# The four sums of each pair of token rows on GpSimd instead of VectorE, in a kernel of three chained matrix products

## The chip, the core and the metric

The kernel runs on one core of a Trainium2 chip. Five engines work side by side, each through its own queue of instructions, in order: TensorE (PE; matmuls, 128 by 128), VectorE (DVE), ScalarE (ACT), GpSimd (POOL) and SyncE (SP, which here only issues DMAs). GpSimd issues DMAs too. The metric is the device time of one execution in microseconds (us).

## What is computed

x is 2048 tokens by 640 channels, fp32. The reference takes the layer norm of x, the real part of its two-dimensional Fourier transform by DFT matrices, and an MLP across the tokens with 1728 hidden units; the sum of x and both is the output:

```python
def _A_ref(x, dft_seq_re, dft_seq_im, dft_hid_re, dft_hid_im):
    a = jnp.einsum("bsd,ed->bse", x, dft_hid_re)
    b = jnp.einsum("bsd,ed->bse", x, dft_hid_im)
    return jnp.einsum("ts,bse->bte", dft_seq_re, a) - jnp.einsum("ts,bse->bte", dft_seq_im, b)

def _B_ref(x, w1, b1, w2, b2):
    h = _layernorm(x, axis=-1)
    u = _gelu(jnp.einsum("bsd,sf->bdf", h, w1) + b1)
    return (jnp.einsum("bdf,fs->bds", u, w2) + b2).transpose(0, 2, 1)

x = A_x
xn = _layernorm(x, axis=-1)
return x + _A_ref(xn, ...) + _B_ref(xn, B_w1, B_b1, B_w2, B_b2)
```

## The kernel before

**Products.** Every fp32 product is made of three matmuls (`three`, lines 158 to 164): each operand is cut into a rounded high part, which ScalarE writes (`high`, line 150), and the remainder, which VectorE subtracts (`low`, line 153); high by high, high by low and low by high are added in PSUM. Besides, blocks of two by two are multiplied with seven products in place of eight, so that sums and differences of blocks are operands as well.

**Stages.** `first_columns` and `columns` multiply the normalized rows of x by the DFT matrices along the tokens and store the result y to DRAM (`store_y`, lines 488 to 492, DMAs issued by GpSimd). `hidden` multiplies y by the DFT along the channels, `up` and `down` are the MLP. The stage of the change is the first, up to about 190 us.

**The fixed operand.** In the first stage the rows of x are the operand that stays in SBUF. There are two halves of eight blocks of 128 token rows. Block q and block q + 4 of a half are a pair, q from 0 to 3, and each pair gets a tile of operands with high and low parts (`fixed[h][q]`; in the lists below n_119 to n_122 for pairs 0 to 3 of the first half, n_1045, n_1266, n_1452 and n_1672 for the second). Of the 640 channels the first 512 go in two quarters of Q = 256 through the seven products, which need four sums of a pair, each of 128 by 256 (`sums_of_rows`, lines 329 to 367). With `row` for block q and `lower` for block q + 4, and 0 and 1 for the quarter, they are, all in place: lower1 = row1 + lower1 (job1, line 342), lower1 = lower1 - row0 (job2), lower0 = lower0 - lower1 (job3), row1 = row0 - row1 (job4); the last three go through the helper `sub` of line 156. After each sum ScalarE copies its high part (`hi`), and at the start of the next job VectorE takes the remainder (`lo`). The second sum overwrites what the first one's remainder reads, so it stands behind that remainder; the others wait for earlier sums alone.

**The order.** Every engine's instructions stand in the order in which the program writes them (`tc.manual_schedule`). The start is a list of words; from step 6 on `turn_of(i, ...)` writes one turn for each step i: loads, reads of PSUM banks, the ScalarE cut of the piece of step i + 2 (a piece is a 128 by 512 block of the DFT matrix, the operand that moves; three buffers), copies of PSUM banks to c tiles and their stores, `jobs` taken from a queue, the VectorE remainder of that piece, more jobs, and last the matmuls of step i. The sums of the first half stand in that queue from step 6 in the order (pair, job) 00 01 10 11 02 12 20 21 30 31 22 32 03 13 and so on, one or two a turn by a table of numbers (`JOBS_AT`). In what follows, a turn is named by its i: turn 11 has the third sum of pair 1, turn 12 the first two of pair 2, turn 14 the first two of pair 3, turn 20 the third sums of pairs 2 and 3. The piece that is cut at the head of turn i + 1, right behind such a turn's last job, belongs to step i + 3. Those of the second half follow from about 110 us on, three neighbouring turns with one sum each behind a first.

Of the kernel before, what the change touches and what calls it, by code (L numbers as in the profile page):

```python
# [77 lines left out]
def fnet_plus_mixer(  # L78
# [30 lines left out]
    nc = tc.nc  # L109
# [39 lines left out]
    def high(hi, src):  # L149
        nc.scalar.activation(hi, src, AF.Copy)  # L150

    def low(lo, src, hi):
        nc.vector.tensor_sub(lo, src, hi.bitcast(F32))  # L153

    def sub(to, a, b):
        nc.vector.tensor_sub(to, a, b)  # L156
# [163 lines left out]
    def part(a, which, i, n=1):  # L320
        return a[:, which, at_slot[i] : at_slot[i] + n * Q]
# [7 lines left out]
    def sums_of_rows(h, q, row, lower, apart=False):  # L329


        def a(of, i):
            return of()[:, i * Q : (i + 1) * Q]

        def hi(i, src):
            high(part(fixed[h][q], 0, i), src)

        def lo(i, src):
            low(part(fixed[h][q], 1, i), src, part(fixed[h][q], 0, i))

        def job1():
            nc.vector.tensor_add(a(lower, 1), a(row, 1), a(lower, 1))
            hi(3, a(lower, 1))

        def job2():
            lo(3, a(lower, 1))
            sub(a(lower, 1), a(lower, 1), a(row, 0))
            hi(4, a(lower, 1))

        def job3():  # L350
            lo(4, a(lower, 1))
            sub(a(lower, 0), a(lower, 0), a(lower, 1))
            hi(5, a(lower, 0))

        def job4():
            lo(5, a(lower, 0))
            sub(a(row, 1), a(row, 0), a(row, 1))
            if not apart:
                job5()

        def job5():
            hi(6, a(row, 1))

        def job6():
            lo(6, a(row, 1))

        return [job1, job2, job3, job4] + [job5] * apart + [job6]


# [934 lines left out]
```

## Time and profile before

| | |
|---|---|
| median of 3 runs | 866.72 us (866.56 to 866.78) |
| span of the profiled execution | 865.1 us, first to last instruction; 1.6 us less than the median |
| TensorE, weight loads | busy 860.7 us, 789.6 us |
| VectorE, ScalarE | busy 695.2 us, 523.0 us |
| GpSimd | busy 158.8 us, of it 195 DMAs issued |
| granted TensorE clock | 1.000 over the span |

The profile gives no time of the profiled execution other than its span. The page gives busy times by engine, the chain of work that ended last and the costliest groups of instructions by line. Besides it the trace answers by view: who waited for whom; a timeline of one engine in a stretch of time (start, duration, engine, line, operation, what is written and read, and in brackets the idle time before and what ended it; "x2" are two instructions in a row, with the time from the first's start to the last's end); busy times by windows. Instructions of ScalarE and VectorE that follow each other overlap by about a tenth of a microsecond in these rows.

### The profile page before, as it was taken

To read this page: it belongs to the slowest core of one execution; us is meant where nothing else is said; L and a number is where in the kernel's file an instruction comes from. 1 tells how busy PE (TensorE), PEld (TensorE's weight loads), DVE (VectorE), ACT (ScalarE), POOL (GpSimd) and SP (SyncE) were. 2 spreads that over 40 slices of the span, in tenths; PEclk is the share of its full clock that TensorE was granted. 3 is DMA by queue.
4 is the path that set the end of the run, shared out by engine and by line. 5 is a ranking of instruction groups with operands and counts; after the bars stand their busy time and mean duration, and the time that the engine had idled before them with its cause. 6 is when DMAs were issued, how large, how long until landed. Compare 5 with 4: busy or idle time off the path is not lost.

```text
span 865.1 us, 13904 instructions
## 1 busy us (share of the span) xinstructions
PE 860.7 (99%) x4899; PEld 789.6 (91%) x4899; DVE 695.2 (80%) x1177; ACT 523.0 (60%) x968; POOL 158.8 (18%) x215
## 2 busy tenths in 40 slices
PE   9999999999999999999999999999999999999998
PEld 6888888888888888889999999999999999999998
DVE  7898868758767888677877788888679978987887
ACT  5765576763555555547565556676667866555654
POOL 2222131210020211122110101111312221101211
PEclk9999999999999999999999999999999999999999
DMA  9949596695382746869576766665687689766776
GB/s 337 366 103 268 186 245 235 160 292 151 94 191 29 199 102 135 212 107 200 125 167 157 163 138 196 189 173 162 142 185 176 146 241 244 183 141 126 157 170 149
DMA packets 90293, 154.44 MB, mean 179 GB/s; under 512 B 9008, under 2 KB 37424, under 8 KB 89968
## 3 DMA queue, kind: packets, MB, share of 16 engines
q0 software_dynamic: 25008, 57.52, 36.1%
q1 hardware_dynamic: 64928, 95.80, 34.0%
q8 instruction: 38, 0.62, 0.3%
q10 hardware_dynamic: 288, 0.25, 0.1%
q14 instruction: 31, 0.25, 0.1%
HBM read 99.96 MB, written 58.82 MB: 184 GB/s over the span
## 4 chain that ended last, share of the span: by engine, by line
PE 99%; DMA 1%; SPq 0%; ACT 0%; DVE 0%; issue 0%; DVEq 0%
PE psum L161 32%; PE psum L162 32%; PE psum L164 31%; PE psum L515 3%; DMA pieces<-in_dft_seq 1%; ACT piece L150 0%; SPq L503 0%; SPq L539 0%; DVE pair L954 0%; DVEq L1300 0%
## 5 line engine op out<-in xcount | busy, mean ns | idle before, releaser
L153 DVE TENSOR_TENSOR piece<-pieces,piece 128x512 fp32r<-128x512 f32 (+4 forms) x496 | 327.2, 660 | 129.8 <-ACT piece L150 125.2
L150 ACT ACTIVATE piece<-pieces 128x512 fp32r<-128x512 f32 (+3 forms) x472 | 295.3, 626 | 224.6 <-PE psum L164 143.0
L161 PE MATMUL psum<-piece,n 128*128 128x512 f32 x540 | 210.3, 389 | 0.0
L164 PE MATMUL psum<-piece,n 128*128 128x512 f32 x540 | 210.3, 389 | 0.0
L162 PE MATMUL psum<-piece,n 128*128 128x512 f32 x540 | 210.3, 389 | 0.0
L162 PE MATMUL psum<-sup,piece 128*128 128x320 f32 x392 | 120.9, 309 | 0.0
L162 PE MATMUL psum<-sdown,piece 128*128 128x320 f32 x392 | 120.9, 309 | 0.0
L161 PE MATMUL psum<-sup,piece 128*128 128x320 f32 x392 | 120.9, 309 | 0.0
L161 PE MATMUL psum<-sdown,piece 128*128 128x320 f32 x392 | 120.9, 309 | 0.0
L162 PEld LDWEIGHTS psum<-piece,n 128*128 128x128 f32 x540 | 101.4, 188 | 21.1
L161 PEld LDWEIGHTS psum<-piece,n 128*128 128x128 f32 x540 | 101.4, 188 | 20.9
L164 PEld LDWEIGHTS psum<-piece,n 128*128 128x128 f32 x540 | 101.4, 188 | 20.9
L156 DVE TENSOR_TENSOR pieces<-pieces 128x512 f32<-128x512 f32 (+3 forms) x142 | 111.9, 793 | 3.0
L164 PE MATMUL psum<-sup,piece 128*128 128x320 f32 x368 | 113.9, 310 | 0.0
L164 PE MATMUL psum<-sdown,piece 128*128 128x320 f32 x368 | 113.9, 310 | 0.0
L492 POOL DMA_DIRECT2D y<-c x65 | 56.0, 898 | 255.2 <-DVE c L691 154.0
L164 PE MATMUL psum<-shid,piece 128*128 128x320 f32 x280 | 86.7, 310 | 0.0
L162 PE MATMUL psum<-shid,piece 128*128 128x320 f32 x280 | 86.7, 309 | 0.0
L161 PE MATMUL psum<-shid,piece 128*128 128x320 f32 x280 | 86.6, 309 | 0.0
L161 PEld LDWEIGHTS psum<-sdown,piece 128*128 128x128 f32 x392 | 73.6, 188 | 0.0
L161 PEld LDWEIGHTS psum<-sup,piece 128*128 128x128 f32 x392 | 73.6, 188 | 0.0
L162 PEld LDWEIGHTS psum<-sup,piece 128*128 128x128 f32 x392 | 73.6, 188 | 0.0
(135 smaller groups left out, 1107.2 us busy)
## 6 DMA issues: line engine op xcount, KB each, us to landing
pieces<-in_dft_seq SPq DMA_DIRECT2D x120, 256.0 KB, 5.4
y<-c POOLq DMA_DIRECT2D x105, 256.0 KB, 4.9
pieces<-in_w SPq DMA_DIRECT2D x88, 256.0 KB, 3.8
out<-pair POOLq DMA_DIRECT2D x36, 320.0 KB, 5.5
pieces<-y SPq DMA_DIRECT2D x32, 320.0 KB, 4.2
pieces<-in_w SPq DMA_DIRECT2D x32, 192.0 KB, 2.6
out<-in_x SPq DMA_DIRECT2D x16, 320.0 KB, 8.8
up<-pair POOLq DMA_DIRECT2D x8, 640.0 KB, 3.2
```

The source lines that it names most:

```text
L150: nc.scalar.activation(hi, src, AF.Copy)
L153: nc.vector.tensor_sub(lo, src, hi.bitcast(F32))
L156: nc.vector.tensor_sub(to, a, b)
L161: nc.tensor.matmul(psum, wh, mh, start=first, stop=False, skip_group_check=True)
L162: nc.tensor.matmul(psum, wh, ml, start=False, stop=last and wl is None, skip_group_check=True)
L164: nc.tensor.matmul(psum, wl, mh, start=False, stop=last, skip_group_check=True)
L492: nc.gpsimd.dma_start(y_part[m][c][:, j, :], t, accum_op=ALU.add)
L515: nc.tensor.matmul(banks[m, j], channels(k, j)[rows], w[cols], start=n == 0 and k == begin, stop=n == 2 and k == end, skip_group_check=True,)
```

## The change

The four sums of every pair are written for GpSimd, with the same operands, at the same places of the program. The helper `sub` stays as it was for all others that use it.

```diff
         def job1():
-            nc.vector.tensor_add(a(lower, 1), a(row, 1), a(lower, 1))
+            nc.gpsimd.tensor_add(a(lower, 1), a(row, 1), a(lower, 1))
             hi(3, a(lower, 1))

         def job2():
             lo(3, a(lower, 1))
-            sub(a(lower, 1), a(lower, 1), a(row, 0))
+            nc.gpsimd.tensor_sub(a(lower, 1), a(lower, 1), a(row, 0))
             hi(4, a(lower, 1))

         def job3():
             lo(4, a(lower, 1))
-            sub(a(lower, 0), a(lower, 0), a(lower, 1))
+            nc.gpsimd.tensor_sub(a(lower, 0), a(lower, 0), a(lower, 1))
             hi(5, a(lower, 0))

         def job4():
             lo(5, a(lower, 0))
-            sub(a(row, 1), a(row, 0), a(row, 1))
+            nc.gpsimd.tensor_sub(a(row, 1), a(row, 0), a(row, 1))
```

32 instructions move, four for each of eight pairs; the lists of TensorE, ScalarE and SyncE stay as they were. On GpSimd, from turn 6 on, there were only stores of y (y_85, y_86, y_89 and y_90 are its blocks in DRAM, c the tiles that are stored). Before:

```order
L490 DMA y_85<-c 128x512 x5
L490 DMA y_89<-c 128x512 x5
L490 DMA y_86<-c 128x512 x3
L492 DMA y_86<-c 128x512 x2
L490 DMA y_90<-c 128x512 x2
```

And with the change, from turn 10 to turn 20 (x_75 holds the first seven blocks of rows, x_76 the eighth):

```order
L352 TENSOR_TENSOR x_75<-x_75 128x256
L490 DMA y_89<-c 128x512 x2
L352 TENSOR_TENSOR x_75<-x_75 128x256
L490 DMA y_89<-c 128x512 x2
L342 TENSOR_TENSOR x_75<-x_75 128x256
L347 TENSOR_TENSOR x_75<-x_75 128x256
L490 DMA y_89<-c 128x512
L490 DMA y_86<-c 128x512 x2
L342 TENSOR_TENSOR x_76<-x_75,x_76 128x256
L347 TENSOR_TENSOR x_76<-x_76,x_75 128x256
L490 DMA y_86<-c 128x512
L492 DMA y_86<-c 128x512
```

The third sum of pair 1 (the second L352) now stands behind two stores, the first sum of pair 2 behind two more, and that of pair 3 behind three.

On VectorE, in turns 12 to 14, the rows that go (pieces_123 and pieces_124 are the raw blocks of the DFT matrix, piece is what is cut of them):

```order
 L153 TENSOR_TENSOR n_121<-x_75,n_121 128x640
-L342 TENSOR_TENSOR x_75<-x_75 128x256
 L153 TENSOR_TENSOR piece<-pieces_123,piece 128x512
 L153 TENSOR_TENSOR n_121<-x_75,n_121 128x256
-L156 TENSOR_TENSOR x_75<-x_75 128x256
 L153 TENSOR_TENSOR piece<-pieces_123,piece 128x512
 L153 TENSOR_TENSOR n_122<-x_76,n_122 128x640
-L342 TENSOR_TENSOR x_76<-x_75,x_76 128x256
 L153 TENSOR_TENSOR piece<-pieces_123,piece 128x512
 L153 TENSOR_TENSOR n_122<-x_76,n_122 128x256
-L156 TENSOR_TENSOR x_76<-x_76,x_75 128x256
 L156 TENSOR_TENSOR pieces_123<-pieces_124,pieces_123 128x1024
```

The remainders and the long sum of the DFT blocks stay where they were, and close up.

In the second half, on GpSimd, the four sums of a pair (here the first; `later` holds its rows) stand between the stores of y:

```order
 L492 DMA y_87<-c 128x512
+L342 TENSOR_TENSOR later<-later 128x256
 L490 DMA y_91<-c 128x512 x2
+L347 TENSOR_TENSOR later<-later 128x256
+L352 TENSOR_TENSOR later<-later 128x256
+L357 TENSOR_TENSOR later<-later 128x256
 L492 DMA y_91<-c 128x512 x4
```

Three of them follow each other there, with no store between.

## The prediction

> **What bounds the kernel now.** I read the page first, its busy times and its chain of what ended last, and then the view of who waited for whom, for TensorE (PE) alone.
>
> ```profile
> span 865.1 us, 13904 instructions
> PE 860.7 (99%) x4899; PEld 789.6 (91%) x4899; DVE 695.2 (80%) x1177; ACT 523.0 (60%) x968; POOL 158.8 (18%) x215
> PE 99%; DMA 1%; SPq 0%; ACT 0%; DVE 0%; issue 0%; DVEq 0%
> ...
> PE psum L147 <- PEq L1293: 0.8, 1, 0.8
> PE psum L515 <- ACT piece L150: 0.3, 1, 0.3
> PE psum L515 <- DVE n L394: 0.2, 1, 0.2
> ```
>
> TensorE is busy for 860.7 of 865.1 us, and in the whole run it waits 1.3 us (0.8 + 0.3 + 0.2), none of it for a sum of a row pair. So nothing that is taken off VectorE (DVE) can shorten the run by more than a few tenths, and every other engine matters through one question alone: does a piece of the DFT matrix, cut by ScalarE (ACT, line 150) and then by VectorE (line 153), still reach TensorE in time? The change is read from the slack of those pieces at the places where the sums stand.
>
> **What is removed and what is added.** 32 sums (four sums, four pairs, two halves) of this kind leave VectorE:
>
> ```profile
> L342 DVE TENSOR_TENSOR x<-x x3: 421/422/425, 25.6 to 38.2; 128x256 f32<-128x256 f32 x3
> ```
>
> 32 x 0.42 us is 13.5 us of VectorE's 695.2, and by the waits above it buys nothing on TensorE. The same 32 sums are added on GpSimd (POOL), where the trace of before has no operation with two inputs. Its nearest rows, with what VectorE did beside them:
>
> ```profile
> 15.09 0.26 POOL L247 TENSOR_SCALAR norm<-mv,norm 128x1 f32<-128x1 f32 x1
> 15.89 0.69 DVE L153 TENSOR_TENSOR piece<-pieces,piece 128x512 fp32r<-128x512 f32 x1
> 15.95 0.84 POOL L258 TENSOR_SCALAR beside<-half,near 128x1 f32<-128x1 f32 x1 [0.23 <-ACT near L236]
> 16.62 0.84 DVE L153 TENSOR_TENSOR n<-x,n 128x640 fp32r<-128x640 f32 x1
> 16.90 0.70 POOL L259 TENSOR_SCALAR norm<-beside,near 128x1 f32<-128x1 f32 x1
> ...
> L1068 POOL MEMSET pair<- 64x640 f32 x1 | 0.6, 627 | 3.1 <-DMA pair<-up 3.1
> L1293 POOL MEMSET const-float32-1.0<- 128x1 f32 x1 | 0.1, 108 | 0.0
> ```
>
> Two things stand there. First a price: one element a partition costs 0.26 us, and a memset grows from 0.108 to 0.627 us between 1 and 640 elements, 0.8 ns an element. A sum of 256 elements reads two inputs and writes one. If all that passes at once it takes 0.26 + 0.21 = 0.47 us; if the two reads pass one after the other, 0.26 + 2 x 0.21 = 0.68; if the write comes on top as well, 0.89. I take 0.70, next to the middle row, with 0.47 and 0.95 as ends. Second, a block: the same one-element work takes 0.26 us at 15.09, but 0.84 at 15.95 and 0.70 at 16.90, and these two end 0.21 and 0.14 us after the VectorE operation with two inputs beside them (15.89 + 0.69 = 16.58; 16.62 + 0.84 = 17.46). So GpSimd stands still while VectorE runs such an operation; I take it that this holds for the sums, and the other way round. [...]
>
> Further handovers: 0.03 us from VectorE to ScalarE (a sum now ends at 41.29 and ScalarE starts at 41.32, below), 0.1 us to GpSimd (L258 ends at 16.79, L259 starts at 16.90). Behind a store I let the sum start at once.
>
> **Where the time goes: turns 11 and 12.** On GpSimd the sums stand in one queue with the stores of y, in the written order, and a store waits for ScalarE's copy of c. ScalarE in turn now waits for the sum, and what is queued behind that wait on ScalarE is the next copies of c and the next piece. As it is before:
>
> ```profile
> 37.45 1.07 POOL L490 DMA_DIRECT2D y<-c  x2 [10.01 <-ACT c L523]
> 37.53 0.42 ACT L150 ACTIVATE n<-x 128x256 fp32r<-128x256 f32 x1
> 38.36 1.08 ACT L523 ACTIVATE c<-psum 128x512 f32<-128x512 f32 x2
> 39.25 1.07 POOL L490 DMA_DIRECT2D y<-c  x2 [0.73 <-ACT c L523]
> 39.31 1.06 ACT L150 ACTIVATE n<-x 128x640 fp32r<-128x640 f32 x2
> 40.40 0.43 DVE L153 TENSOR_TENSOR n<-x,n 128x256 fp32r<-128x256 f32 x1 [1.21 <-ACT n L150]
> 40.86 0.43 DVE L156 TENSOR_TENSOR x<-x 128x256 f32<-128x256 f32 x1
> 41.32 0.42 ACT L150 ACTIVATE n<-x 128x256 fp32r<-128x256 f32 x1 [0.95 <-DVE x L156]
> 42.30 0.69 DVE L153 TENSOR_TENSOR piece<-pieces,piece 128x512 fp32r<-128x512 f32 x1 [1.00 <-ACT piece L150]
> 43.86 0.39 PE L162 MATMUL psum<-piece,n 128*128 128x512 f32 x1
> ```
>
> Now the same with the sums on GpSimd. The third sum of pair 1 (L352) stands behind the two stores: 37.45 + 1.07 = 38.52, + 0.70 = 39.22. ScalarE's copy at 37.53 reads it and moves to 39.25, 1.72 late. The two copies of c behind it move from 38.36 to 40.08, their stores from 39.25 to 40.97, which end at 42.04. Behind them stands the first sum of pair 2 (L342): it ends at 42.74. The second copy of the row at 39.31 started at 39.95 (39.31 + 1.06 - 0.42); it moves to 42.77, 2.82 late. VectorE's remainder moves from 40.40 to 43.22 and ends at 43.65; the second sum (L347) starts at 43.75 and ends at 44.45; ScalarE goes on at 44.48 instead of 41.32, 3.16 late. The piece behind it and its remainder are late by as much: 42.30 becomes 45.46. That remainder ended at 42.99 and TensorE wanted it at 43.86, a slack of 0.87. TensorE stands still for 3.16 - 0.87 = **2.3 us**.
>
> **Turn 14.** The pattern comes again with pair 3:
>
> ```profile
> 44.05 1.07 POOL L490 DMA_DIRECT2D y<-c  x2 [0.46 <-ACT c L679]
> 44.22 0.42 ACT L150 ACTIVATE n<-x 128x256 fp32r<-128x256 f32 x1
> 44.70 0.42 DVE L153 TENSOR_TENSOR n<-x,n 128x256 fp32r<-128x256 f32 x1
> 45.50 1.22 DVE L156 TENSOR_TENSOR pieces<-pieces,pieces 128x1024 f32<-128x1024 f32 x1
> 45.62 0.42 ACT L150 ACTIVATE n<-x 128x256 fp32r<-128x256 f32 x1 [0.98 <-DVE x L156]
> 46.63 0.69 DVE L153 TENSOR_TENSOR piece<-pieces,piece 128x512 fp32r<-128x512 f32 x1
> 47.94 0.39 PE L162 MATMUL psum<-piece,n 128*128 128x512 f32 x1
> ```
>
> With 3.16 us of lateness the stores start at 47.21 and end at 48.28, the sum ends at 48.98, ScalarE's 44.22 becomes 49.01 and VectorE's 44.70 becomes 49.49, ending at 49.91. VectorE goes straight on to its sum of 128x1024, 1.22 us, begun about 0.08 us before that end, so until 51.05. GpSimd asks at 50.01 and finds it running: blocked for 1.04 us, it ends at 51.75. ScalarE goes on at 51.78 instead of 45.62, 6.16 late. The slack of this piece is 47.94 - 47.32 = 0.62, so TensorE is 5.54 late by here: **3.25 us** more, or 2.2 if nothing blocks.
>
> **Turn 20 and the rest.**
>
> ```profile
> 55.51 0.91 POOL L492 DMA_DIRECT2D y<-c  x1 [7.63 <-ACT n L150]
> 56.13 1.22 DVE L156 TENSOR_TENSOR pieces<-pieces,pieces 128x1024 f32<-128x1024 f32 x1
> 56.25 0.42 ACT L150 ACTIVATE n<-x 128x256 fp32r<-128x256 f32 x1 [0.74 <-DVE x L156]
> 57.26 0.69 DVE L153 TENSOR_TENSOR piece<-pieces,piece 128x512 fp32r<-128x512 f32 x1
> 59.50 0.39 PE L162 MATMUL psum<-piece,n 128*128 128x512 f32 x1
> ...
> 118.67 0.69 DVE L153 TENSOR_TENSOR piece<-pieces,piece 128x512 fp32r<-128x512 f32 x1
> 120.70 0.39 PE L162 MATMUL psum<-piece,n 128*128 128x512 f32 x1
> ```
>
> Everything comes 5.54 later. The store goes from 55.51 to 61.05 and lets GpSimd go half a store's time later, about 61.6; by then VectorE is in the sum that stood at 56.13 (61.67 to 62.89), and two sums follow, until 64.29. ScalarE's second copy moves from 56.25 to 64.32, 8.07 late; the piece's slack is 59.50 - 57.95 = 1.55; TensorE is 6.5 late: **0.95 us** more. Without a block the two sums would fit into the slack. In the second half (sums from 111 to 185 us) the slack of a piece is like that at 118.67: 120.70 - 119.36 = 1.34 us, against three sums in neighbouring turns, each some 0.45 us dearer than now (0.28 of length, 0.1 to 0.2 of handover), 1.35 together. That is the edge, where I put **0.5 us** for the four pairs and what is left of the first half; at 0.95 us a sum, each pair loses 0.75 more, 3.0 in all, and at 0.47 nothing.
>
> The sum is 2.3 + 3.25 + 0.95 + 0.5 = 7.0 us on the profiled execution's span of 865.1; around it lie 1.6 us to the median of 866.7, which I keep. **Forecast: 873.7 us.** The ends: sums of 0.47 and no block give (2.3 - 3 x 0.23) + (2.2 - 2 x 0.23) = 3.35, 870.1; sums of 0.95 with the block give (2.3 + 0.75) + (3.25 + 0.5) + (0.95 + 0.5) + 3.5 = 11.75, 878.5.
>
> **The rivals.** *Not slower.* VectorE, with 32 operations less, has the pieces ready earlier, and ScalarE's waits for sums vanish in its idle time. It decides if GpSimd could start each sum where VectorE did. Against it: with a sum of no length at all, turns 11 and 12 still give 38.52 to 38.55 (1.02 late), stores ending at 41.34, ScalarE at 41.37, remainder until 42.25 and ScalarE at 42.38, 1.06 late against a slack of 0.87. It would give 866.5, since only the waits of 0.3 and 0.2 could go. Chance 0.05, of it 0.02 for faster.
>
> *No block between the two engines.* What stretched the rows at 15.95 and 16.90 is some other thing, or does not hold for long operations. Then turns 12 and 14 alone cost, 2.3 + 2.2 = 4.5: 871.2 us. The equal ends of operations speak against it. Chance 0.2.
>
> *Sums near a microsecond.* Nothing in the trace shows two inputs on GpSimd; the 0.95 end, 878.5 us. Chance 0.2.
>
> *The granted clock falls.* The view by windows (busy time of each engine, then the granted clock) has it at 1.00 everywhere but in the last microsecond:
>
> ```profile
> 861.00:862.30 1.30, 0.92 (x7) 0.66 (x5) 1.01 (x4) 0.00 (x0) 0.00 (x0) 1.00 0.82 289
> ...
> 864.00:865.00 1.00, 0.00 (x0) 0.00 (x0) 0.00 (x0) 0.00 (x0) 0.00 (x0) 0.81 0.00 0
> ```
>
> The last matmul ends near 862.0, so two to three microseconds without one are enough for a fall. In turn 14 TensorE would stand still for some 2.7 us of the 3.25 in one go. A fall there would cost an estimated 1 to 3 us, by how low and how long: 876 us. Against it: that the fall came only behind 864. [...] Chance 0.1.
>
> **How the numbers follow.** That leaves 0.45 for the forecast's own case. The range is **870 to 881**: from the end with short sums and no block, to long sums with one fall of the clock on top; what lies outside is the case that is not slower (0.05) and sums well over a microsecond (about 0.1). A run of this kernel tells changes of over 0.2% (1.7 us) from none; so faster 0.02, the same 0.03, slower 0.95.
>
> **What would show it.** Right: TensorE gets waits of 2 to 3 us each on line 150 or 153 near 44 and 50 us, ScalarE waits for GpSimd's sums, the clock stays full, and behind 200 us all runs as before, only later. The sums' rows would read near 0.7 us, and longer where VectorE was busy with two inputs. Wrong: no waits on TensorE before 60 us, sums that start beside VectorE's operations without stretching them, or a loss that sits mostly in the second half.

## The result and the profile after

| | before | with the change |
|---|---|---|
| median | 866.75 us (866.56 to 866.93, 4 runs) | 876.0 us (875.81 to 877.4, 4 runs) |
| span of the profiled execution | 865.1 us | 875.6 us (its own time: 877.4 us) |
| granted TensorE clock, mean | 1.000 | 0.997 |

The ratio is 1.0111 (95% interval 1.0099 to 1.0123): 9.25 us slower. The profiled execution is the slowest of the four; the other three took 875.8 to 876.1 us, and where that difference comes from is shown below.

The page of the changed kernel: busy times, and the chain of what ended last.

```profile
span 875.6 us, 13900 instructions
PE 865.3 (99%) x4899; PEld 789.6 (90%) x4899; DVE 694.6 (79%) x1145; ACT 521.2 (60%) x968; POOL 186.5 (21%) x247
PE 89%; DVE 5%; ACT 3%; POOL 1%; issue 1%; DMA 1%; SPq 0%; ACTq 0%; DVEq 0%; POOLq 0%
```

VectorE lost 32 instructions (1177 to 1145) but only 0.6 us of busy time, where 13.5 us left: the rest of its work got longer by nearly as much. GpSimd gained 27.7 us with them, 0.87 us a sum. In the chain, where TensorE stood alone, DVE, ACT and POOL now hold 9% of the span; that says where the chain runs, not how much was lost.

Who waited for whom, TensorE alone (us in total, times, longest):

```profile
PE psum L161 <- ACT piece L150: 4.3, 2, 2.3
PE psum L162 <- DVE piece L153: 1.4, 5, 0.3
...
PE psum L515 <- DVE n L394: 0.7, 1, 0.7
```

The two new waits on line 161, of 1.97 and 2.32 us below, are for a piece's high part, which ScalarE cuts (line 150). The wait on line 515 has nothing to do with the sums: it stands at 5.72 us, the first sum runs at 27.76, and TensorE had made it up by 7.1 us. The timeline of turns 11 to 14 with the change, engine by engine, shows what ScalarE was doing:

```profile
38.17 1.10 POOL L490 DMA_DIRECT2D y<-c  x2 [2.84 <-ACT c L523]
39.29 0.75 POOL L352 TENSOR_TENSOR x<-x 128x256 f32<-128x256 f32 x1
40.07 0.42 ACT L150 ACTIVATE n<-x 128x256 fp32r<-128x256 f32 x1 [1.71 <-POOL x L352]
41.79 1.10 POOL L490 DMA_DIRECT2D y<-c  x2 [1.75 <-ACT c L523]
42.91 0.75 POOL L342 TENSOR_TENSOR x<-x 128x256 f32<-128x256 f32 x1
44.64 0.72 POOL L347 TENSOR_TENSOR x<-x 128x256 f32<-128x256 f32 x1 [0.99 <-DVE n L153]
45.40 0.42 ACT L150 ACTIVATE n<-x 128x256 fp32r<-128x256 f32 x1 [1.29 <-POOL x L347]
46.36 0.69 DVE L153 TENSOR_TENSOR piece<-pieces,piece 128x512 fp32r<-128x512 f32 x1 [1.80 <-ACT piece L150]
46.38 0.50 PE L161 MATMUL psum<-piece,n 128*128 128x512 f32 x1 [1.97 <-ACT piece L150]
47.11 0.50 PE L162 MATMUL psum<-piece,n 128*128 128x512 f32 x1 [0.22 <-DVE piece L153]
...
48.12 1.07 POOL L490 DMA_DIRECT2D y<-c  x2 [0.45 <-ACT c L679]
49.21 0.75 POOL L342 TENSOR_TENSOR x<-x,x 128x256 f32<-128x256 f32 x1
50.78 1.22 DVE L156 TENSOR_TENSOR pieces<-pieces,pieces 128x1024 f32<-128x1024 f32 x1
50.94 1.64 POOL L347 TENSOR_TENSOR x<-x,x 128x256 f32<-128x256 f32 x1 [0.99 <-DVE n L153]
52.61 0.42 ACT L150 ACTIVATE n<-x 128x256 fp32r<-128x256 f32 x1 [2.20 <-POOL x L347]
53.60 0.49 PE L161 MATMUL psum<-piece,n 128*128 128x512 f32 x1 [2.32 <-ACT piece L150]
54.33 0.50 PE L162 MATMUL psum<-piece,n 128*128 128x512 f32 x1 [0.23 <-DVE piece L153]
```

A sum starts 0.02 us behind its stores and takes 0.72 to 0.75 us where nothing hinders it, and ScalarE picks it up 0.03 to 0.04 us later. The L347 at 50.94 asks 0.16 us behind the start of VectorE's sum of 128x1024, and ends at 52.58, which is 0.58 us after that one's end at 52.00. The same stretch of the granted clock, in windows (from:to, length, then the busy time of PE, PE's weight loads, DVE, ACT and POOL, each with its number of instructions, then the clock, DMA share, GB/s):

```profile
45.05:48.47 3.42, 1.86 (x7) 1.32 (x8) 2.03 (x3) 2.92 (x6) 1.22 (x3) 1.00 0.07 29
...
51.88:55.29 3.41, 1.46 (x5) 1.02 (x6) 1.83 (x3) 2.46 (x5) 1.26 (x2) 1.00 0.00 0
55.29:58.71 3.42, 3.42 (x9) 2.65 (x9) 3.42 (x5) 0.63 (x1) 0.00 (x0) 0.50 0.23 81
```

Behind turn 14's stand the clock is granted at half for 3.42 us, in which TensorE is busy throughout and gets through 9 matmuls. Last, where the lateness of TensorE stands further on, by one matmul at each place:

```profile
36.20 0.50 PE L162 MATMUL psum<-piece,n 128*128 128x512 f32 x1
67.76 0.50 PE L162 MATMUL psum<-piece,n 128*128 128x512 f32 x1
71.08 0.50 PE L162 MATMUL psum<-piece,n 128*128 128x512 f32 x1 [0.31 <-DVE piece L153]
...
130.45 0.50 PE L162 MATMUL psum<-piece,n 128*128 128x512 f32 x1 [0.30 <-DVE piece L153]
180.07 0.50 PE L162 MATMUL psum<-piece,n 128*128 128x512 f32 x1 [0.33 <-DVE piece L153]
```

Against the same matmuls before, the lateness of TensorE is:

| matmul (line 162) | before | with the change | late | predicted |
|---|---|---|---|---|
| ahead of turn 12 | 35.70 | 36.20 | 0.50 | 0 |
| behind turn 12 | 43.86 | 47.11 | 3.25 | 2.3 |
| behind turn 14 | 47.94 | 54.33 | 6.39 | 5.54 |
| behind turn 20 | 59.50 | 67.76 | 8.26 (with the clock's fall) | 6.5 |
| two steps later | 62.22 | 71.08 | 8.86 | |
| second half, first | 120.70 | 130.45 | 9.75 | |
| second half, last | 169.66 | 180.07 | 10.41 | 7.0 |

From there to the end nothing more is lost: the spans differ by 10.5.

### The profile page after: what moved, and what is told of

It is laid out like the page before. It is cut to its first block, busy times and chain, and to the rows that moved or that the text cites. A ratio compares the mean times of both kernels' runs of the same rounds, so it can differ in the third digit from the quotient of the medians.

```text
span 875.6 us, 13900 instructions
## 1 busy us (share of the span) xinstructions
PE 865.3 (99%) x4899; PEld 789.6 (90%) x4899; DVE 694.6 (79%) x1145; ACT 521.2 (60%) x968; POOL 186.5 (21%) x247
## 4 chain that ended last, share of the span: by engine, by line
PE 89%; DVE 5%; ACT 3%; POOL 1%; issue 1%; DMA 1%; SPq 0%; ACTq 0%; DVEq 0%; POOLq 0%
PE psum L162 30%; PE psum L161 30%; PE psum L164 29%; DVE piece L153 2%; ACT piece L150 1%; DVE pieces L156 1%; DVE n L153 1%; DVE st L227 1%; DMA later<-in_x 1%; POOL y L490 0%; ACT c L679 0%; POOL x L347 0%; ACT n L150 0%; ACT c L523 0%; DMA x<-in_x 0%
## 5 line engine op out<-in xcount | busy, mean ns | idle before, releaser
L153 DVE TENSOR_TENSOR piece<-pieces,piece 128x512 fp32r<-128x512 f32 (+4 forms) x496 | 333.2, 672 | 133.8 <-ACT piece L150 131.4
L161 PEld LDWEIGHTS psum<-sup,piece 128*128 128x128 f32 x392 | 73.6, 188 | 0.0
L161 PEld LDWEIGHTS psum<-sdown,piece 128*128 128x128 f32 x392 | 73.6, 188 | 0.0
L162 PEld LDWEIGHTS psum<-sdown,piece 128*128 128x128 f32 x392 | 73.6, 188 | 0.0
```

Source lines behind the costliest of these rows:

```text
L161: nc.tensor.matmul(psum, wh, mh, start=first, stop=False, skip_group_check=True)
L162: nc.tensor.matmul(psum, wh, ml, start=False, stop=last and wl is None, skip_group_check=True)
```

## The experiments

The theory: sums wait in GpSimd's queue behind stores of y, and sums and VectorE's operations with two inputs hold each other up; each makes ScalarE, and with it the cut of the piece, late. Rivals: the sum's mere length; GpSimd's writes as such; the fall of the clock; the second half. Each run is compared with the kernel before on the same chip (866.63 to 866.66 us there). The diffs give the lines that matter, against the changed kernel. Where a place in a run is called late, its matmuls are set against the same matmuls before.

**The change again.**

> The changed kernel once more, for its clock. In its profile the granted clock fell to half for 3.4 us at 55.05 us, right behind a stand of TensorE of 2.5 us, and eight matmuls took 0.43 instead of 0.23 us: 1.6 us of the 10.5 by which that span grew. If the fall belongs to the stall (clock theory), this profile has it again, at the same place, and the time is 876 again. If it was chance, the profile has no fall and its span is near 874.0 (865.1 + 8.9).

876.56 us (875.71 to 877.3), ratio 1.0108 (1.0093 to 1.0124). The clock fell at the same stand, from 55.21 to 58.62. Over both sets of four runs, three took 877.3 to 877.4 us and five 875.7 to 876.1; one of the five, 875.85 us, had a mean clock of 1.000. So a fall behind turn 14 goes with some 1.5 us, but not in every execution.

**Either half alone.** The engine is chosen by half (here the first; the other kernel has `h == 1`):

```diff
+        def on(j):
+            return nc.gpsimd if h == 0 else nc.vector
-            nc.gpsimd.tensor_add(a(lower, 1), a(row, 1), a(lower, 1))
+            on(1).tensor_add(a(lower, 1), a(row, 1), a(lower, 1))
```

> Sums of the first half on GpSimd, of the second on VectorE. TensorE's lateness in the changed kernel grows by 9.1 us up to 70 us and by 1.4 us behind (0.7 each at 120 and 170). If the two halves are independent, 876.0 - 1.4 = 874.6. If the lateness of the second half comes from what the first leaves behind, VectorE's sums there change nothing: 876.

> Sums of the second half on GpSimd, of the first on VectorE. Independent halves: 866.75 + 1.4 = 868.1, with waits of TensorE at 120 and 170 us alone. If they depend on each other: 866.8.

First half: 875.24 us, ratio 1.0097 (1.0083 to 1.011), 8.6 us. Second half: 867.99 us, ratio 1.0015 (1.0006 to 1.0024), 1.3 us. The first half is most of it. It took 0.6 us more than expected, and the two profiles show where. Up to 110 us both kernels have the same instructions in the same order, but the second sum of pair 1 (line 347, here 350) meets two remainders of VectorE, and the two engines shared the time differently: first the change, then the first half alone.

```profile
33.33 1.11 POOL L347 TENSOR_TENSOR x<-x 128x256 f32<-128x256 f32 x1 [1.93 <-DVE n L153]
34.48 0.42 ACT L150 ACTIVATE n<-x 128x256 fp32r<-128x256 f32 x1 [1.98 <-POOL x L347]
...
33.36 1.66 POOL L350 TENSOR_TENSOR x<-x 128x256 f32<-128x256 f32 x1 [1.94 <-DVE n L153]
```

In the change the two remainders take 1.70 us together and the sum 1.11; in the other 0.62 and 1.66. ScalarE gets the sum 0.55 us later there, and ahead of turn 12 TensorE is 1.18 us late instead of 0.62 (the matmul that stood at 37.97 before stands at 39.15 and at 38.59).

What the second half costs is a block the other way round, as the timeline of the second kernel shows (its lines stand three further down: L360 is the fourth sum):

```profile
119.47 0.92 POOL L360 TENSOR_TENSOR later<-later 128x256 f32<-128x256 f32 x1
119.72 1.22 DVE L153 TENSOR_TENSOR piece<-pieces,piece 128x512 fp32r<-128x512 f32 x1
121.00 0.50 PE L162 MATMUL psum<-piece,n 128*128 128x512 f32 x1 [0.30 <-DVE piece L153]
```

VectorE's remainder takes 1.22 us in place of 0.69, beside GpSimd's sums, and the matmul that stood at 120.70 waits.

**Stores behind the sums.** Stores of y are kept back and written behind the jobs of their turn, in all turns:

```diff
+        held_stores.append((lambda: put_y(add, m, c, j, t), t))
...
+        put_stores()
```

> All sums on GpSimd, but each turn's stores of y are written behind its jobs. Queue theory (most of the loss comes from sums that stand behind stores, which wait for ScalarE, which waits for the sum before): the sums of turns 11 and 12 come in time, ScalarE goes on about 0.4 us late against a slack of 0.87, so no wait there; in turn 14 the block by the long VectorE sum remains, 1.3 us late against 0.62, so 0.7; no fall of the clock; second half 1.4: 866.75 + 2.1 = 868.9. Rival (length and block do it without the queue): near 876, with the same two large waits.

872.82 us, ratio 1.0072 (1.0059 to 1.0085): 3.2 us gained over the change, but 3.9 less than expected. The wait of turn 12 is gone. But TensorE is already 2.3 us late ahead of it, turn 14 costs 1.6 us in place of 0.7, and some 0.7 us more goes between there and 70 us. The timeline of the start:

```profile
29.61 2.92 POOL L503 DMA_DIRECT2D y<-c  x5
32.55 0.75 POOL L342 TENSOR_TENSOR x<-x 128x256 f32<-128x256 f32 x1
33.33 0.42 ACT L150 ACTIVATE n<-x 128x256 fp32r<-128x256 f32 x1 [2.69 <-POOL x L342]
```

Five stores that stood ahead of all sums now stand ahead of pair 1's first one, and ScalarE waits 2.69 us for it. So the move was made again from turn 11 on only, with the sums on VectorE as a control, and with GpSimd:

> Control: the kernel before, sums on VectorE, with each turn's stores of y written behind its jobs from turn 11 on. 866.7 if the order of the stores matters only together with sums on GpSimd; over 867.5 if the later stores cost something by themselves.

> All sums on GpSimd, stores behind the jobs from turn 11 on only, so that the five stores of turn 6 no longer stand ahead of pair 1's first sum. If what was left in the run with all stores last (two waits of 1.0 us near 34) came from those five stores: 872.8 - 2.1 + 0.5 (the start as in the changed kernel) = 871.2, no wait at turn 12, and at turn 14 the block by the long VectorE sum. If that lateness comes back at turn 14 anyway: 872.8.

Before with later stores: 866.67 us, ratio 1.0000 (0.9991 to 1.0008). The change with later stores: 871.54 us, ratio 1.0056 (1.0043 to 1.007). The stores' place costs nothing by itself and 4.5 us with the sums on GpSimd: 876.0 - 871.5. What is left in turn 14, 1.6 us, is the block alone, with no store ahead of the sums:

```profile
45.00 1.12 POOL L342 TENSOR_TENSOR x<-x,x 128x256 f32<-128x256 f32 x1 [0.23 <-DVE n L153]
46.94 1.22 DVE L156 TENSOR_TENSOR pieces<-pieces,pieces 128x1024 f32<-128x1024 f32 x1
47.10 1.65 POOL L347 TENSOR_TENSOR x<-x,x 128x256 f32<-128x256 f32 x1 [0.99 <-DVE n L153]
49.78 0.49 PE L161 MATMUL psum<-piece,n 128*128 128x512 f32 x1 [0.94 <-ACT piece L150]
```

**Sums that read nothing.** Each sum becomes two memsets of the same tile, so that GpSimd is nearly as long at work but only writes, and the sums themselves are left out; first at the change's places, then with later stores:

```diff
-            nc.gpsimd.tensor_add(a(lower, 1), a(row, 1), a(lower, 1))
+            nc.gpsimd.memset(a(lower, 1), 0.01)
+            nc.gpsimd.memset(a(lower, 1), 0.02)
```

> Each GpSimd sum is replaced by two memsets of its result, 128x256 each: GpSimd is busy for about as long (2 x 0.3 us) but reads nothing, and the sums themselves are left out. Block theory (GpSimd stands still while VectorE reads two inputs): no such operation lasts longer than 0.4 us, turn 14 gets 1.1 us less, turn 20 and the second half lose nothing, no fall of the clock: 876.0 - 1.1 - 0.9 - 1.4 - 1.6 = 871. Without a block: as in the changed kernel less some 0.15 us a sum, 874 to 875, and memsets near VectorE's 128x1024 sum would be stretched to 1.6 us as that sum was.

> As the run before, with each sum replaced by two memsets of its result (the sums are left out): neither queue nor block, only the length and the handovers to GpSimd. Queue and block together being the cause: 866.7 + 0.5 to 1.0 = 867.5. If length and handovers by themselves cost much: over 869.

871.46 us, ratio 1.0055 (1.0043 to 1.0068); with later stores 867.12 us, ratio 1.0005 (0.9996 to 1.0014). The timeline of the first, in turn 14:

```profile
49.68 1.22 DVE L156 TENSOR_TENSOR pieces<-pieces,pieces 128x1024 f32<-128x1024 f32 x1
49.82 0.31 POOL L348 MEMSET x<- 128x256 f32 x1 [0.97 <-DVE n L153]
50.19 0.31 POOL L349 MEMSET x<- 128x256 f32 x1
```

The two memsets together take 0.68 us, little less than an unhindered sum, and run beside the very operation that stretches the sum to 1.64. So the block goes with GpSimd's reading in these runs. Put together, in medians:

| | stores where they were | stores later |
|---|---|---|
| sums on VectorE | 866.7 | 866.7 |
| two memsets on GpSimd | 871.5 | 867.1 |
| sums on GpSimd | 876.0 | 871.5 |

The queue costs 4.3 to 4.5 us in the second row and the third. In both columns the sums cost 4.4 to 4.5 more than memsets, which is the block between the engines and the 0.07 us by which an unhindered sum is longer; in turn 12, where no sum was stretched, that length is worth some 0.3 us. The two add up to all but 0.4 to 0.5 us, the length and handovers of the last corner, which the interval there doesn't tell from nothing.

**Half the length.** Each sum takes the first 128 of its 256 columns (`[:, :P]` behind each operand); the other half of it is left out.

> The GpSimd sums work on 128 of their 256 columns; the other half of each sum is left out. Length theory: a sum falls from 0.74 to some 0.5 us, which saves 3 x 0.24 in turn 12, 2 x 0.24 in turn 14, and the stand in turn 14 falls from 2.5 to about 1.3 us, too short for the clock; the second half loses nothing: 876.0 - 0.7 - 0.5 - 1.6 - 1.4 - 0.8 (turn 20 and start) = 871. If the length hardly matters (queue and block alone): 875 to 876.

871.5 us, ratio 1.0059 (1.0046 to 1.0071). Two sums of its timeline:

```profile
41.72 0.48 POOL L342 TENSOR_TENSOR x<-x 128x128 f32<-128x128 f32 x1
48.97 1.37 POOL L347 TENSOR_TENSOR x<-x,x 128x128 f32<-128x128 f32 x1 [0.99 <-DVE n L153]
```

An unhindered sum falls from 0.75 to 0.48 us, the one beside VectorE's long operation from 1.64 to 1.37: the block adds 0.89 us to either. TensorE still stands in turns 12 and 14 (2.5 us on line 161 against 4.3), and the second half costs nothing: 0.27 us a sum brings it back under its slack. The 4.5 us gained are as much as the queue or the block is worth. So length is cheap by itself (the corner of the table above) and dear where queue and block hand it on: the three causes don't simply add.

**Pair 3's first two sums on VectorE again.**

```diff
+            return nc.gpsimd if not (h == 0 and q == 3 and j <= 2) else nc.vector
```

> The first two sums of pair 3 (first half; turn 14) back on VectorE, the other 30 on GpSimd. That takes both the queue and the 1.64 us long blocked sum out of turn 14. Expected: the wait at turn 12 (2.75 us) stays, that at turn 14 (3.1 us) goes, and the clock's fall (1.6 us) with it: 876.0 - 4.7 = 871.3. If the lateness only moves to turn 20, less than half of it is saved: 874 or more.

873.21 us, ratio 1.0078 (1.0066 to 1.0091): 2.8 us gained of a turn that held 3.1, less than expected by 1.9. Of turn 14's stand 0.2 us is left. Most of what is missing is the 1.6 us for the clock, which the median of the change hardly holds (next experiment). About 0.3 us comes back later, where lateness had given cover: behind turn 20, at 63.68 us in its timeline, TensorE loses 0.6 us, where it lost 0.1 in the change.

**The clock.** Eight matmuls of constants are put ahead of the matmuls of step 17, whose piece is late in turn 14; then ahead of those of steps 15 and 17:

```diff
+        if i in (15, 17):
+            for _ in range(8):
+                nc.tensor.matmul(psum[0], idle[:, :P], idle, start=True, stop=True)
```

> The changed kernel with eight matmuls on constants before the matmuls of step 17, where TensorE stands still in turn 14; their PSUM bank is free there. They take 8 x 0.22 = 1.7 us of a wait of 2.3 us, so they delay nothing. Clock theory: the stand falls below 1 us, the clock stays full and the 1.6 us of the fall are saved: 874.4. If the fall isn't due to that stand, or isn't in most executions: 876.0.

> The changed kernel with eight matmuls on constants before the matmuls of step 15 as well as of step 17, so that TensorE doesn't stand still for long at either place. Seen so far: in the grid of 3.41 us on which the clock's stretches begin and end, a fall followed each stretch with 2.2 us or more without matmuls, and none with 1.8 or less. Clock theory: no fall in any run, and what is left are the waits: 866.7 + 8.9 = 875.6 in all runs, the profile's span near 874.0. If the fall is not decided by these stands: a fall in the profile again, span near 875.5.

One place: 876.0 us (875.88 to 876.16), ratio 1.0107 (1.0092 to 1.0123), no gain on the median. In its profile the clock fell behind turn 12's stand instead (47.64 to 51.05 us). Two places: 875.86 us (875.83 to 875.88), ratio 1.0105 (1.0091 to 1.0119), with a mean clock of 0.999 to 1.000 and no run at 877. The one execution of the changed kernel with a mean clock of 1.000 took as long, 875.85. So without any fall the change costs 9.2 us, and a fall behind turn 12 costs next to nothing: 0.1 us between these two runs, and as little between the executions of the memset kernel (871.46 to 871.53 us at a mean clock of 0.998, 871.36 and 871.39 at 1.000). Why, the kernel with the first half alone shows, whose clock fell there too:

```profile
46.96 0.50 PE L161 MATMUL psum<-piece,n 128*128 128x512 f32 x1 [1.98 <-ACT piece L150]
54.18 0.50 PE L161 MATMUL psum<-piece,n 128*128 128x512 f32 x1 [0.73 <-ACT piece L150]
...
44.68:48.09 3.41, 1.21 (x5) 0.55 (x4) 1.58 (x3) 2.12 (x5) 1.13 (x2) 1.00 0.11 43
48.09:51.50 3.41, 3.41 (x10) 2.67 (x9) 1.38 (x4) 1.21 (x3) 1.97 (x4) 0.50 0.61 231
```

From the one stand's end to the other's are 7.22 us, as in the changed kernel with a full clock between them (46.38 to 53.60). The slow matmuls only use up the wait that follows: 0.73 us is left of 2.32. Behind turn 14 no such wait follows, and there the fall is paid for. Three expectations above (half the length, memsets, pair 3) took 1.6 us for the clock off a median that holds some 0.15 of it. That two of them came within 0.5 us is luck: other terms were larger than expected by about as much.

## Why the prediction was right, and where it was short

**Direction, places and mechanism held.** TensorE got two stands, of 2.2 us up to 47.11 and 2.6 us up to 54.33 (lines 161 and 162 together); ScalarE waited for GpSimd's sums; sums stretched beside VectorE's operations with two inputs; and most of the loss, 5.9 us, sits in turns 11 to 14. The table above shows the two causes apart: queue 4.3 to 4.5 us, block (with a little length) 4.4 to 4.5. The rivals *not slower* and *no block* fall with it. One of the signs of being right didn't come: the clock didn't stay full.

**The sum was 7.0 us, the medians say 9.25.** Term by term, from the profiled execution:

- *Ahead of turn 12: priced at nothing, 0.50.* The sums of pairs 0 and 1, from 27.76 us on, already made pieces late: TensorE was 0.1 us early ahead of them and 0.50 late by 36.20. ScalarE had waited until 34.48 for the second sum of pair 1 (row above). From there it works without a gap up to the copies of c that the stores of turn 11 wait for, so turn 11 began at 38.17 and not at 37.45, 0.72 late. This is the step that failed first: the walk started at turn 11 with everything on time.
- *Turn 12: 2.3, measured 3.25 - 0.50 = 2.75.* The walk itself was nearly right. ScalarE went on at 45.40 instead of 41.32, 4.08 late: 0.72 from the start and 3.36 for the 3.16 that I had, since a sum took 0.75 us for my 0.70, a pair of stores 1.10 for 1.07, and a sum started 0.02 behind its stores. The remainder began at 46.36 instead of 42.30, 4.06 late; its slack is 0.81 and not 0.87, since 0.06 lie between its end and the matmul; 4.06 - 0.81 = 3.25. The list of waits names line 161 because the high part is asked for first, but the remainder, as priced, sets the lateness.
- *Turn 14: 3.25, measured 6.39 - 3.25 = 3.14.* The working holds almost link by link: I had GpSimd blocked for 1.04 us and ending at 51.75, measured were 0.89 us and 52.58, with the whole walk 0.8 us late from ahead.
- *The clock: a rival at 0.1.* It fell, in a full window of 3.41 us, and cost about 1.6 (eight matmuls of 0.43 us in place of 0.23) of the 8.26 - 6.39 = 1.87 us that the profiled execution lost between turns 14 and 20. I had argued from the fall seen at the end of the program before, and given a stand of 2.7 us a chance of 0.1 to bring one; waits of 2.32 and 0.23 us did. That a fall would cost 1 to 3 us was my estimate, which no row of before showed, since no matmul follows the fall there. In the median it is small, since five of the eight executions took 876.1 us or less: against 875.86 without a fall it makes 0.15 of the first median and 0.7 of the repeated one.
- *Turn 20: 0.95, measured about 0.3 up to there, 0.6 two steps on and 0.4 up to the second half.* That the size is near is luck. The block that I had walked, on the third sums, was nearly covered by the slack; the 0.6 came from two remainders of VectorE at 69.86, 2.31 us in place of 1.39, beside the fourth sums.
- *Second half and rest: 0.5, measured 1.2* (0.6 each at 120 and 170 us of before; 1.3 in the kernel that changes it alone). I had let sums be dearer by 0.45 us; I had not let VectorE's remainders be blocked by them, 1.22 us in place of 0.69 at 119.72 in that kernel, though I had taken the block to hold both ways.

0.5 + 2.75 + 3.14 + 1.6 + 1.3 + 1.2 = 10.5 us, the profiled difference, and 8.9 without the clock. An execution without a fall has a span of 874.1 us, 9.0 above the profiled one of before; that one was 0.2 longer than the median span of the kernel before (864.9), which makes the 9.2 of the medians. The mechanism was right; the terms at both ends were too small, and the lateness from the start came through turn 12.

**A sum's length** was put at 0.70 with ends 0.47 and 0.95. By the profile 15 of the 32 take 0.72 to 0.76 us, 16 take 0.87 to 1.25, and the one of turn 14 takes 1.64. Most of the longer ones stand beside an operation of VectorE with two inputs. Three of 1.05 to 1.08 us begin inside the end of a store, where a memset, too, takes 0.3 us more. So the value was close, and its dear end, *sums near a microsecond*, describes the hindered ones.

**What stays open.** How the two engines take turns when both have work queued. The prediction let the later one wait until the earlier one is done, and turn 14 agrees; this row of the change does not:

```profile
63.83 3.27 DVE L156 TENSOR_TENSOR pieces<-pieces,pieces 128x1024 f32<-128x1024 f32 x1
```

It began 0.40 us ahead of two sums, which took 1.08 us each and were both done before it; no run took that apart. Nor is it known how often the meeting near 33 us goes the other way; of seven traces in which it takes place, that of the first half alone is the only one. There it accounts for 0.56 of the 0.65 us by which the halves, 8.6 and 1.3, add to more than the whole. No version with sums on GpSimd came below the kernel before: its TensorE has 1.3 us of waits to give, and the best of them that computes everything for both halves stands at 871.54.

## What to carry to other kernels

Before work is moved to an engine that looks idle, read what stands in its queue at that place: here half the loss is sums standing behind stores which wait for something else. Walk the chain from the first moved instruction, not from the first one that looks dangerous, since the 0.7 us from small early steps arrived undiminished at the tight place. And moving work off VectorE, which did not bound the time, bought nothing, while any consumer in between (here ScalarE's in-order queue) can carry each delay on to the engine that does.

## What the runs showed of the hardware

**Where TensorE had little work in a stretch of 3.41 us, the next one ran at half clock.** In the changed kernel's trace the clock falls to 0.50 at 55.29 us, for 3.41 us, and again at 874.49, 819.20 us later, which is 240 times as long: falls lie on a grid. Its place differs from run to run: in the second profile of the change the fall begins at 55.21. A grid window in which TensorE was busy for 1.21 us (first half alone, above), 1.46 (the change, above) or 1.68 was followed by a whole one at 0.50; windows with 1.86 (the change, at 45.05), 1.89 (half-length sums, at 50.05) and 2.11 (stores behind the sums in all turns, at 31.84) were followed by 1.00. Where the programs end it is the same: windows with 1.41 us (the change, from 871.07) and 0.71 (before, from 861.21) were followed by 0.50. The row of 1.68, from the memsets at the change's places, with the window behind it:

```profile
43.34:46.75 3.41, 1.68 (x7) 0.85 (x6) 1.67 (x4) 2.38 (x6) 1.17 (x3) 1.00 0.33 135
46.75:50.17 3.42, 3.42 (x10) 2.65 (x9) 1.45 (x4) 0.95 (x3) 2.02 (x5) 0.50 0.61 230
```

In these rows the two kinds part between 1.68 and 1.86 of 3.41 us, about half. The expectation of the two-place run, a fall with 2.2 us or more without matmuls and none with 1.8 or less, was off: the window of 1.68 has 1.73 without, that of the change 1.95. Whether a stand of 2 us brings a fall went with where it lies in the grid: with 1.97 us in turn 12 of the change (window of 1.86) there was none, with 1.98 in the kernel of the first half alone (window of 1.21) there was one. That could explain why one kernel took 875.8 and 877.3 us, but of its executions near 875.8 there is no trace.

**Sums of GpSimd and two-input operations of VectorE stretched each other; memsets of GpSimd kept their length.** Beside VectorE's sum of 128x1024 a sum of GpSimd took 1.64 us in place of 0.72 to 0.75 (the change, at 50.94), and beside sums VectorE's remainder took 1.22 in place of 0.69 (second half alone, at 119.72). Two memsets of 128x256 took 0.31 us each beside the same 128x1024 operation (at 49.82 and 50.19, above). (In the run at the change's places 59 of 64 take 0.31 to 0.34 us; four that begin inside the end of a store take 0.63 to 0.67, and one takes 0.54, at 29.84. In the change the sum there, at 29.65, took 1.04 beside an operation of VectorE that reads one tile and scalars, line 573.) Small operations were stretched too: one of 128x2 takes 0.69 us beside a sum, where its neighbours take 0.16.

```profile
27.76 0.87 POOL L342 TENSOR_TENSOR x<-x 128x256 f32<-128x256 f32 x1
27.96 0.69 DVE L242 SCALAR_TENSOR_TENSOR r<-mv,near 128x2 f32<-128x2 f32 x1
28.68 0.16 DVE L243 SCALAR_TENSOR_TENSOR r<-r,near 128x2 f32<-128x2 f32 x1
```
